# Attention scored over pairs of heads, 64 queries of each per tile, in a fused attention and two-MoE kernel

## The chip, the cores and the metric

The kernel runs on one core of a Trainium2 chip. The metric is device time in microseconds: 1187.81 us is the median of three runs of the kernel before (1185.43 to 1188.58). Engines are called as the profile calls them: PE is the matrix engine, PEld its weight loads, DVE the vector engine, ACT the scalar engine, POOL the third elementwise engine, and SP the engine that issues all DMAs here. Each engine works through its own list of instructions in order, so an instruction that waits holds up everything behind it on that engine.

## The reference, cut to what matters

Causal attention in blocks of 64 positions over 4 batches of 8 heads, 576 positions and head size 64, then two gated layers (512 to 1536 to 512) over all 2304 tokens.

```python
scores = (1/sqrt(64)) * q @ k.T                     # per head, 576 x 576
mask = (pos[:, None] // 64) >= (pos[None, :] // 64) # whole 64-blocks
attn = softmax(where(mask, scores, -1e9))           # row maximum taken off first
x = attn @ v                                        # -> (2304, 512)
x = (x @ w_a) * (x @ w_b) @ w_out                   # layer 1
xn = x / rms(x) * rms_g                             # layer 2
out = silu(xn @ w_gate) * (xn @ w_val) @ w_out2
```

## The kernel before

**Numbers in two halves.** float32 matmuls are made of matmuls in the type F32R. A float32 operand is split in a high part (a copy in F32R) and a low part (the operand less the copy). The two layers (`moe`, L444 to L446 and L471 to L473) use three products per tile. Products of two plain F32 operands also occur: for the eight heads of batch 0 ("plain" heads) the values are not split and L375 works on F32.

**Attention, head by head.** `score(m, i)` takes 128 queries (64 in the last of five tiles) against all keys up to the last that any of them may see: 128, 256, 384, 512 and 576 keys (576 in two halves of 288). Queries (`qh`, `ql`) and keys (`kk`) are split by `make_qk` (L252 to L258); since the head size is 64, `kk` holds the high part of the keys in one half of its 128 rows and the low part in the other. Each score tile is two matmuls (L289 with `qh`, L290 with `ql`) into a PSUM tile `s` (or `mm`). DVE writes the masked value over the 64 by 64 corner that the earlier 64 queries may not see (L293) and reduces the row maximum (L295; L298 and L299 for halves). ACT takes the exponential and its row sum (L301). L311 and L312 make reciprocals of the sums, and POOL scales the probabilities `p` (L315). `p_transposes` turns them in 128 by 128 pieces (L336, with `ident` or `swap`), and the result leaves PSUM as a high part `ph` (ACT, L353) and a low part `pl` (DVE, L354); for plain heads as one copy. `values` multiplies with the values `vv` (L375) and adds up the two halves into `xf` (L386, L387).

**Weights.** They arrive as 64-bit words in 72 pieces of 512 KB. `prepare()` takes a piece: a load into a staging tile `st` (three buffers, `stage_loads`, L154), `decode` on ACT, DVE and POOL (L131 to L135), a split (L97, L107) and a write of the result to DRAM, from where later blocks fetch it (L188, L192). The pieces of layer 1 are all decoded before or during the first token block, those of layer 2 in the background of blocks 1 to 4.

**Order.** First attention of batch 0 runs alone, with nine weight pieces between its steps. Then five token blocks of layer 1 follow (512, then four times 448 tokens; 432 matmuls each), then the five of layer 2. Attention of batches 1 to 3 is mixed into blocks 0 to 2: after each step of `moe` the attention stream is stepped while its accounted cost is below a share (`PACE`) of that of the block, with a higher priority (`AHEAD`). Attention that the next block needs and that isn't issued by the last part of a block is issued there in one go (`before_last`). A scheduler then orders each engine's list by priority and by when it takes operands to be ready, so the lists differ from the order of the code.

Of the kernel before, what the change touches and what calls it, by code (L numbers as in the profile page):

```python
# [17 lines left out]
MASKED = -1000000000.0  # L18
# [5 lines left out]
Q_HI = "aad"  # L24
# [22 lines left out]
def tile_attention_moe_moe(  # L47
# [40 lines left out]
    swap = const.tile([P, P], F32, name="swap")  # L88
# [60 lines left out]
    def stage_loads(n):  # L149
        while len(staged) + prepared[0] < min(n, len(w_pieces)):  # L150
            i = len(staged) + prepared[0]
            layer, kind, f, y = w_pieces[i]
            st = stage.tile([P, 4 * P], I64, tag="st", name="st", bufs=3)
            sp.dma_start(out=st, in_=(w_ab if kind == "ab" else w_o)[layer][f, y])  # L154
            staged[i] = st

    def prepare():
# [4 lines left out]
        stage_loads(i + 3)  # L162
# [27 lines left out]
    def fetch_o(layer, i):  # L190
# [13 lines left out]
    ]  # L204
    PLACE, PART = {}, [0, 0]
    for part, pieces in GROUPS:
        for j, i in pieces:
            PLACE.setdefault(j, (part, PART[part]))
            PART[part] += tw(i)

    def attention(pools, x_of, done):

        ap, ap2, ps_s, ps_t = pools
        NH = B * H
        n_copy = [0]
        q_raw, k_raw, v_raw, qk, vv, pp, st, pt = {}, {}, {}, {}, {}, {}, {}, {}

        def rows(m):
            hh = m % 2
            return slice(hh * D, hh * D + D), slice(D - hh * D, P - hh * D)  # L220

        def plain(m):

            return m < H

        def load(m):
            if m >= NH:
                return
            b, h = divmod(m, H)
            if h % 2 == 0:  # L230
                t = ap2.tile([P, S], F32, tag="kr", name="kr", bufs=1)
                sp.dma_start(out=t, in_=k[b, h // 2])
                k_raw[m] = k_raw[m + 1] = t
            t = ap2.tile([P, S], F32, tag="qr", name="qr")
            sp.dma_start(out=t[0:D, :], in_=q[b, h])
            sp.dma_start(out=t[D:P, :], in_=q[b, h])
            q_raw[m] = t
            t = ap2.tile([P, NTILE, D], F32, tag="vr", name="vr")
            sp.dma_start(out=t[:, 0:LAST_TILE, :], in_=v[b, h][:, 0:LAST_TILE, :])

            sp.dma_start(out=t[P - R:P, LAST_TILE, :], in_=v[b, h][0:R, LAST_TILE, :])
            sp.dma_start(out=t[0:P - R, LAST_TILE, :], in_=v[b, h][R:P, LAST_TILE, :])
            v_raw[m] = t

        def make_qk(m):
            if m >= NH:
                return
            r, z = rows(m)
            qr, kr = q_raw.pop(m), k_raw.pop(m)
            qh = ap2.tile([P, S], F32R, tag="qh", name="qh")  # L250
            kk = ap2.tile([P, S], F32R, tag="kk", name="kk")
            act.activation(kk[r, :], kr[r, :], AF.Copy, scale=SCALE)  # L252
            copy(eng[Q_HI[min(m // H, len(Q_HI) - 1)]], qh, qr)
# [5 lines left out]
            qk[m] = (qh, ql, kk)  # L259

        def make_vv(m):
            if m >= NH:
                return
            t = v_raw.pop(m)
            if plain(m):
                vv[m] = t
                return
            o = ap2.tile([P, NTILE, P], F32R, tag="vv", name="vv")
            hi, lo = o[:, :, 0:D], o[:, :, D:P]
            copy(pool, hi, t)  # L270
            pool.tensor_tensor(lo, t, hi.bitcast(F32), ALU.subtract)
            vv[m] = o

        def score(m, i):

            qh, ql, kk = qk[m]
            w = tw(i)
            nk = i * P + w
            o = nk - P
            if m not in st:  # L280
                st[m] = ap2.tile([P, 16], F32, tag="st", name="st")
            s = st[m]
            pi = ap2.tile([P, nk], F32, tag=f"p{i}", name=f"p{i}")
            pp[m, i] = pi
# [7 lines left out]
            if w == P:  # L292
                dve.memset(pss[-1][0:64, nk - 64 - halves[-1][0]:nk - halves[-1][0]], MASKED)  # L293
            if len(halves) == 1:
                dve.tensor_reduce(s[:, i:i + 1], pss[0][:, 0:nk], axis=AX.X, op=ALU.max, negate=True)  # L295
            else:
                for x, (a, z) in enumerate(halves):
                    dve.tensor_reduce(s[:, 14 + x:15 + x], pss[x][:, 0:z - a], axis=AX.X, op=ALU.max)  # L298
                dve.tensor_reduce(s[:, i:i + 1], s[:, 14:16], axis=AX.X, op=ALU.max, negate=True)  # L299
            for x, (a, z) in enumerate(halves):  # L300
                act.activation(  # L301
                    pi[:, a:z], pss[x][:, 0:z - a], AF.Exp, bias=s[:, i:i + 1], scale=1.0,
                    accum_out=s[:, 5 + i + x:6 + i + x],
                )
# [11 lines left out]
            return sum(2 * max(107.0, (z - a) / 2.4) for a, z in halves)

        def p_transposes(m):
            pt[m] = []
            at = [0, 0]  # L320
            for part, pieces in GROUPS:
                ps = ps_t()
                n, cost = 0, 0.0
                first, rest = [], []
                for j, i in pieces:

                    if tw(i) == P:
                        rest.append((n, j, i, ident))
                    elif n >= P - R:
                        first.append((n - (P - R), j, i, ident))  # L330
                    else:
                        first.append((n, j, i, swap))
                    n += tw(i)
                for o, j, i, perm in first + rest:
                    a = min(j * P, S - P)
                    pe.transpose(ps[:, o:o + P], pp[m, i][:, a:a + P], perm)  # L336
                    cost += P / 1.2
                if at[part] == 0:
                    kinds = ["hl"[m % 2]] if plain(m) else "hl"
                    dt = F32 if plain(m) else F32R  # L340
                    pt[m].append(
                        [ap.tile([P, PART[part]], dt, tag=f"p{x}{part}", name=f"p{x}{part}") for x in kinds]
                    )
                both = [t[:, at[part]:at[part] + n] for t in pt[m][part]]
                at[part] += n
                if plain(m):
                    n_copy[0] += 1
                    if n_copy[0] % 2 == 0:
                        dve.tensor_copy(both[0], ps[:, 0:n])
                    else:  # L350
                        gate["act"] = act.activation(both[0], ps[:, 0:n], AF.Copy)
                else:
                    gate["act"] = act.activation(both[0], ps[:, 0:n], AF.Copy)  # L353
                    dve.tensor_tensor(both[1], ps[:, 0:n], both[0].bitcast(F32), ALU.subtract)  # L354
                yield cost
            for i in tiles:
                del pp[m, i]

        def values(m):
            b, h = divmod(m, H)  # L360
            p = h // 2
            x = x_of(b)
            r, z = rows(m)
            cost = 0.0
            for a, e in ((0, R), (R, S)):
                ps = ps_t()
                seq = []
                for j in tiles:
                    q0 = max(a, j * P)
                    if q0 < e:  # L370
                        part, n = PLACE[j]
# [348 lines left out]
```

## Time and profile before

| | |
|---|---|
| median of 3 runs | 1187.81 us |
| the profiled execution | 1193.02 us, of which the span is 1191.2 us |
| PE busy | 1132.8 us, 95% of the span |
| DVE, ACT, POOL busy | 710.1, 529.5 and 489.1 us (60, 44 and 41%) |
| mean granted clock of PE | 0.97 of full |

The span is best read by position in the PE list. Counting the matmuls of the layers (L444 to L446, L471 to L473), the 48th starts at 111.62 us, the 432nd is done at 270.77 (end of token block 0), the 864th at 395.80 (block 1), the 912th at 429.65, the 1344th at 563.75 and the 1440th at 589.55. The last attention matmul lies ahead of the 1344th. From 589.55 to the end there is no attention.

### The profile page before, as it was taken

Reading aid. Unit: us, or ns where it says so; the run is one execution under the profiler, and the core shown is the slowest. Engines: PE = TensorE matmul, PEld = TensorE weight load, DVE = VectorE, ACT = ScalarE, POOL = GpSimd, SP = SyncE. Lnnn points to the kernel's source line nnn. Section 1 sums busy time; section 2 is a strip of 40 time slices with the busy share of each in tenths; the row PEclk is TensorE's granted clock in tenths of the full one; section 3 lists DMA queues with packets and bytes.
Section 4 is the critical chain, followed back from the end, with each engine's and each line's share of the span. In section 5 each row is a group of like instructions: output and inputs, shape, how many; then the busy total and the mean of one; then the engine's idle time right before and its main releaser. Section 6 shows DMA issues by size and latency. Waiting matters only on the chain.

```text
span 1191.2 us, 16081 instructions
## 1 busy us (share of the span) xinstructions
PE 1132.8 (95%) x5578; PEld 992.0 (83%) x5578; DVE 710.1 (60%) x1411; ACT 529.5 (44%) x1174; POOL 489.1 (41%) x474
## 2 busy tenths in 40 slices
PE   7888888989999889998999999999999999999998
PEld 5566667769989779898899998888999999999997
DVE  7869799997777787778945523323624534433222
ACT  7758776765655666556533312312312312211211
POOL 6748767776636565546535202112012112112110
PEclk9898988999999889999899999999999999999999
DMA  5436575879777667658898956655765765765760
GB/s 177 147 113 217 192 260 173 311 251 335 261 239 240 229 234 234 230 203 309 310 412 323 341 198 246 224 195 191 279 228 198 280 221 204 256 214 209 255 227 35
DMA packets 65905, 279.98 MB, mean 235 GB/s; under 512 B 12064, under 2 KB 22304, under 8 KB 45344
## 3 DMA queue, kind: packets, MB, share of 16 engines
q1 hardware_dynamic: 65824, 278.95, 66.3%
q8 instruction: 44, 0.72, 0.2%
q14 instruction: 37, 0.30, 0.1%
HBM read 231.74 MB, written 47.19 MB: 234 GB/s over the span
## 4 chain that ended last, share of the span: by engine, by line
PE 67%; DVE 9%; ACT 4%; DMA 3%; POOL 2%; issue 2%; DVEq 0%; POOLq 0%; ACTq 0%
PE mm L445 14%; PE mm L446 14%; PE mm L444 14%; PE mm L471 7%; PE mm L472 7%; PE mm L473 7%; PE t L336 2%; PE t L375 2%; POOL x L135 1%; DVE kk L254 1%; DVE x L133 1%; PE s L289 1%; DVE st L134 1%; PE s L290 1%; DVE pl L354 1%
## 5 line engine op out<-in xcount | busy, mean ns | idle before, releaser
L444 PE MATMUL mm<-xh,ab 128*128 128x448 f32 (+1 forms) x960 | 360.2, 377 | 6.1 <-DVE xf L387 2.1
L446 PE MATMUL mm<-xh,ab 128*128 128x448 f32 (+1 forms) x960 | 358.7, 374 | 0.3 <-POOL ab L107 0.2
L445 PE MATMUL mm<-xl,ab 128*128 128x448 f32 (+1 forms) x960 | 358.3, 373 | 0.0
L107 POOL TENSOR_TENSOR hl<-g,hh 128x448 fp32r<-128x448 f32 (+1 forms) x80 | 99.4, 1243 | 425.1 <-ACT hh L97 424.5
L444 PEld LDWEIGHTS mm<-xh,ab 128*128 128x128 f32 x960 | 181.5, 189 | 26.3 <-ACT ab L97 2.9
L446 PEld LDWEIGHTS mm<-xh,ab 128*128 128x128 f32 x960 | 181.6, 189 | 19.9 <-POOL ab L107 0.4
L445 PEld LDWEIGHTS mm<-xl,ab 128*128 128x128 f32 x960 | 181.9, 190 | 18.3
L471 PE MATMUL mm<-hh,o 128*128 128x448 f32 (+1 forms) x480 | 182.3, 381 | 5.0 <-ACT hh L97 3.5
L472 PE MATMUL mm<-hh,o 128*128 128x448 f32 (+1 forms) x480 | 179.4, 374 | 0.0
L473 PE MATMUL mm<-hl,o 128*128 128x448 f32 (+1 forms) x480 | 169.1, 374 | 0.9 <-POOL hl L107 0.9
L97 ACT ACTIVATE hh<-g 128x448 fp32r<-128x448 f32 (+1 forms) x120 | 70.5, 588 | 204.2 <-DVE g L456 203.7
L315 POOL TENSOR_SCALAR p<-p,st 128x128 f32<-128x128 f32 (+4 forms) x160 | 106.5, 677 | 106.4 <-DVE st L312 63.9
L456 DVE SCALAR_TENSOR_TENSOR g<-mm,asb 128x448 f32<-128x448 f32 (+1 forms) x120 | 76.1, 635 | 117.5 <-PE mm L446 116.6
L135 POOL TENSOR_TENSOR x<-x,st 128x512 uint32<-128x512 uint32 x72 | 104.9, 1461 | 70.3 <-DVE st L134 27.1
L453 DVE SCALAR_TENSOR_TENSOR asb<-mm,asb 128x448 f32<-128x448 f32 (+1 forms) x60 | 38.2, 636 | 144.7 <-ACT asb L452 144.7
L301 ACT ACTIVATE p<-s,st 128x128 f32<-128x128 f32 (+2 forms) x171 | 88.5, 520 | 69.3 <-DVE st L295 40.7
L481 DVE SCALAR_TENSOR_TENSOR acc<-mm,acc 128x448 f32<-128x448 f32 (+1 forms) x120 | 69.9, 627 | 70.6 <-PE mm L473 70.5
L471 PEld LDWEIGHTS mm<-hh,o 128*128 128x128 f32 x480 | 90.9, 190 | 18.2 <-ACT hh L97 5.3
L473 PEld LDWEIGHTS mm<-hl,o 128*128 128x128 f32 x480 | 90.3, 189 | 11.7 <-POOL hl L107 1.7
L452 ACT ACTIVATE asb<-mm 128x448 f32<-128x448 f32 (+1 forms) x60 | 33.4, 556 | 148.1 <-PE mm L446 148.1
L472 PEld LDWEIGHTS mm<-hh,o 128*128 128x128 f32 x480 | 91.3, 190 | 9.1
L336 PE MATMUL t<-ident,p 128*128 128x128 f32 x416 | 73.2, 295 | 3.1 <-POOL p L315 2.9
(99 smaller groups left out, 1645.2 us busy)
## 6 DMA issues: line engine op xcount, KB each, us to landing
ab<-wab SPq DMA_DIRECT2D x108, 1024.0 KB, 6.0
o<-wo SPq DMA_DIRECT2D x36, 1536.0 KB, 6.9
st<-in_w_ab_dram SPq DMA_DIRECT2D x48, 512.0 KB, 4.5
wab<-ab SPq DMA_DIRECT2D x12, 1024.0 KB, 4.5
st<-in_w_o_dram SPq DMA_DIRECT2D x24, 512.0 KB, 4.9
wab<-bg SPq DMA_DIRECT2D x24, 512.0 KB, 7.0
qr<-in_q_dram SPq DMA_DIRECT2D x64, 144.0 KB, 3.8
wo<-o SPq DMA_DIRECT2D x4, 1536.0 KB, 6.2
```

Of the source, the lines that this page charges most:

```text
L107: eng_lo.tensor_tensor(lo, src, hi.bitcast(F32), ALU.subtract)
L135: pool.tensor_tensor(x, x, lo, ALU.add)
L301: act.activation(pi[:, a:z], pss[x][:, 0:z - a], AF.Exp, bias=s[:, i:i + 1], scale=1.0, accum_out=s[:, 5 + i + x:6 + i + x],)
L315: pool.tensor_scalar(pi, pi, s[:, 5 + y:6 + y], 1.0, ALU.mult, ALU.mult)
L336: pe.transpose(ps[:, o:o + P], pp[m, i][:, a:a + P], perm)
L444: pe.matmul(ps[:, 0:n], wh[:, a:z], xh[:, c, 0:n], start=(c == 0), stop=False)
L445: pe.matmul(ps[:, 0:n], wh[:, a:z], xl[:, c, 0:n], start=False, stop=False)
L446: pe.matmul(ps[:, 0:n], wl[:, a:z], xh[:, c, 0:n], start=False, stop=(c == KC - 1))
L456: dve.scalar_tensor_tensor(g, ps[:, 0:n], UNSCALE, asb, ALU.mult, ALU.mult)
L471: pe.matmul(ps[:, 0:n], wh, hh, start=(y == 0), stop=False)
L472: pe.matmul(ps[:, 0:n], wl, hh, start=False, stop=False)
L473: pe.matmul(ps[:, 0:n], wh, hl, start=False, stop=(y == TF - 1))
```

## The change

Two neighbouring heads are scored together. A tile now holds 64 queries of one head and the same 64 queries of the other, in `qz`: rows 0 to 63 hold the first head's queries with zeros in the second head's columns, and rows 64 to 127 the reverse, so that one matmul against the keys of both heads (128 rows) scores both. Nine tiles per pair (64 to 576 keys) take the place of ten; all 128 rows of a tile see the same keys, so there is no mask. Scores are single F32 matmuls: queries and keys are not split. Queries arrive in runs of 64 numbers. The probability tiles `pp` are allocated once. A pair is worked in two parts (query blocks 0 to 5, and 6 to 8), the values of all batches are split, and 25 pieces per pair are transposed, where it was 30. The staging tile `st` has two buffers, and in the first stage a weight piece is prepared at every 9th step.

```diff
-            st = stage.tile([P, 4 * P], I64, tag="st", name="st", bufs=3)
+            st = stage.tile([P, 4 * P], I64, tag="st", name="st", bufs=2)
...
-        stage_loads(i + 3)
+        stage_loads(i + 2)
...
+    Q = P // 2
+    NQ = S // Q
+    PARTS = (range(0, 6), range(6, NQ))
+    SCORED = (tuple(PARTS[0]), (NQ - 1, *range(6, NQ - 1)))
+    NORM = ({3: (0, 4), 5: (4, 6)}, {NQ - 1: (NQ - 1, NQ), NQ - 2: (6, NQ - 1)})
...
+        PLACE.append([(j, b) for j in range(NTILE) for b in blocks_of(part, j)])
...
+        qz = [ap.tile([P, NQ, 2, Q], F32, name=f"qz{x}") for x in range(2)]
...
+        pp = [ap.tile([P, P * (b // 2 + 1)], F32, name=f"pp{b}") for b in range(NQ)]
...
-            sp.dma_start(out=t[0:D, :], in_=q[b, h])
-            sp.dma_start(out=t[D:P, :], in_=q[b, h])
+            for hh in range(2):
+                sp.dma_start(
+                    out=qz[m % 2][hh * D:hh * D + D, :, hh, :],
+                    in_=q[b, 2 * h + hh].rearrange("d (n q) -> d n q", q=Q),
+                )
...
-            dve.scalar_tensor_tensor(
-                kk[z, :], kr[r, :], SCALE, kk[r, :].bitcast(F32), ALU.mult, ALU.subtract
-            )
-            ql = ap2.tile([P, S], F32R, tag="ql", name="ql")
-            pool.tensor_tensor(ql, qr, qh.bitcast(F32), ALU.subtract)
+            t = ks[m] = ap2.tile([P, S], F32, tag="ks", name="ks")
+            act.activation(t, k_raw.pop(m), AF.Copy, scale=SCALE)
...
-                pe.matmul(ps[:, 0:z - a], qh[:, o:nk], kk[:, a:z], start=True, stop=False)
-                pe.matmul(ps[:, 0:z - a], ql[:, o:nk], kk[:, a:z], start=False, stop=True)
+                pe.matmul(ps[:, 0:z - a], qz[m % 2][:, b], ks[m][:, a:z], start=True, stop=True)
...
-                dve.memset(pss[-1][0:64, nk - 64 - halves[-1][0]:nk - halves[-1][0]], MASKED)
...
+                for x, (j, b) in enumerate(group):
+                    pe.transpose(ps[:, x * P:(x + 1) * P], pp[b][:, j * P:(j + 1) * P], ident)
+                n = len(group) * P
+                hi, lo = [t[:, at * P:at * P + n] for t in pt[u]]
+                gate["act"] = act.activation(hi, ps[:, 0:n], AF.Copy)
+                dve.tensor_tensor(lo, ps[:, 0:n], hi.bitcast(F32), ALU.subtract)
...
+                        for t in pt[u]:
+                            t = t.rearrange("p (n h q) -> p n h q", h=2, q=Q)
+                            seq.append((t[:, at:at + len(bs), hh, :], j, (bs[0] - b0) * Q))
...
+                    pe.matmul(
+                        ps[:, o:n], vv[m][:, hh, j, :], src, start=(y == 0), stop=(y == len(seq) - 1)
+                    )
...
-        if n % 16 == 15 and prepared[0] < 2 * TF + TF:
+        if n % 9 == 8 and prepared[0] < 2 * TF + TF:
```

In the changed kernel the score matmul is L263, the transpose L298, the values matmul L324, the layer matmuls L390 to L392 and L417 to L419, and the load of `st` L151.

The first place is the PE list early in token block 2 (after the 888th matmul of the layers). In the kernel before, nine rows there are the end of a product of the layer, transposes and the scores of the next head, each tile twice:

```order
L446 MATMUL mm<-xh,ab 128x448
L336 MATMUL t<-ident,p_4365 128x128
L336 MATMUL t<-ident,p_4395 128x128
L289 MATMUL s<-kk,qh 128x128
L290 MATMUL s<-kk,ql 128x128
L289 MATMUL s<-kk,qh 128x256
L290 MATMUL s<-kk,ql 128x256
L289 MATMUL s<-kk,qh 128x384
L290 MATMUL s<-kk,ql 128x384
```

In the changed kernel, at the same place in block 2 (after the 881st):

```order
L298 MATMUL t<-ident,pp_138 128x128
L298 MATMUL t<-ident,pp_139 128x128
L298 MATMUL t<-ident,pp_140 128x128
L298 MATMUL t<-ident,pp_141 128x128
L263 MATMUL s<-ks,qz_133 128x448
L263 MATMUL s<-ks,qz_133 128x512
L392 MATMUL mm<-xh,ab 128x448
L390 MATMUL mm<-xh,ab 128x448
L391 MATMUL mm<-xl,ab 128x448
```

A score tile is one row where it was two, and two tiles stand between transposes and products of the layer. Between the 864th and the 912th matmul of the layers the PE list held 26 score matmuls, 30 transposes and 13 value matmuls; now it holds 4, 12 and 20.

The second place is the SP list in token block 0, where weights are loaded and decoded. Before, around the fourth write of a decoded weight (`wab_3`):

```order
L154 DMA st<-in_w_ab_dram 128x512
L232 DMA kr<-in_k_dram 128x576
L154 DMA st<-in_w_o_dram 128x512
L235 DMA qr<-in_q_dram 64x576
L236 DMA qr<-in_q_dram 64x576
L180 DMA wab_3_73<-ab 128x2048
L154 DMA st<-in_w_ab_dram 128x512 x2
```

Now, around the same write:

```order
L235 DMA kr<-in_k_dram 128x576
L238 DMA vr<-in_v_dram 128x320 x2
L151 DMA st<-in_w_o_dram 128x512
L151 DMA st<-in_w_ab_dram 128x512
L177 DMA wab_3_73<-ab 128x2048
L151 DMA st<-in_w_ab_dram 128x512
L151 DMA st<-in_w_o_dram 128x512
```

The loads of weights stand closer together, and a load of `st` now waits for the tile two loads earlier to be decoded, where it waited for the tile three loads earlier. Over the whole program the lists have 985 rows on DVE (1286 before), 834 on ACT (888), 343 on POOL (399) and 343 on SP (460).

## Rows read from the trace of the kernel before

**Rows 1.** Windows, whole core by stage: busy us (count) of PE PEld DVE ACT POOL, PEclk, DMA, GB/s

```profile
0.00:111.62 111.62, 91.30 (x412) 64.00 (x412) 88.88 (x247) 81.61 (x207) 75.15 (x85) 0.89 0.50 160
111.62:270.77 159.15, 141.42 (x661) 111.95 (x660) 144.33 (x281) 110.13 (x250) 119.88 (x108) 0.94 0.68 238
270.77:395.80 125.03, 124.17 (x699) 114.74 (x698) 93.41 (x228) 73.54 (x186) 72.69 (x81) 1.00 0.75 261
395.80:429.65 33.85, 26.14 (x118) 21.97 (x117) 23.28 (x61) 20.64 (x52) 19.69 (x24) 0.80 0.62 213
429.65:563.75 134.10, 129.27 (x710) 116.95 (x709) 104.19 (x232) 79.32 (x195) 74.91 (x81) 0.99 0.72 249
563.75:589.55 25.80, 23.24 (x99) 20.25 (x97) 23.95 (x24) 13.83 (x25) 13.32 (x10) 0.87 0.82 300
589.55:1191.20 601.65, 597.23 (x2889) 542.12 (x2887) 232.02 (x343) 150.38 (x264) 113.42 (x89) 1.00 0.66 238
```
**Rows 2.** Timeline of PE in block 1: start us, us, engine, line, operation, count

```profile
280.12 0.37 PE L444 MATMUL mm<-xh,ab 128*128 128x448 f32 x1
...
282.76 0.37 PE L445 MATMUL mm<-xl,ab 128*128 128x448 f32 x1
...
284.00 0.39 PE L375 MATMUL t<-ph,vv 128*128 128x512 f32 x1
...
284.66 0.30 PE L289 MATMUL s<-kk,qh 128*128 128x288 f32 x1
...
284.93 0.37 PE L375 MATMUL t<-pl,vv 128*128 128x448 f32 x1
...
285.79 0.44 PE L336 MATMUL t<-ident,p 128*128 128x128 f32 x2
...
296.29 1.14 PE L336 MATMUL t<-ident,p 128*128 128x128 f32 x9
...
297.27 0.27 PE L336 MATMUL t<-swap,p 128*128 128x128 f32 x1
...
298.14 0.39 PE L289 MATMUL s<-kk,qh 128*128 128x512 f32 x1
...
298.60 0.36 PE L473 MATMUL mm<-hl,o 128*128 128x448 f32 x1
```
**Rows 3.** Timeline of PE, values of a plain head of batch 0

```profile
77.59 2.80 PE L375 MATMUL t<-ph,vr 128*64 128x512 f32 x10
80.32 0.44 PE L336 MATMUL t<-ident,p 128*128 128x128 f32 x2
```
**Rows 4.** Timeline of PE at the start of block 2, the wait ahead in brackets

```profile
405.18 0.33 PE L289 MATMUL s<-kk,qh 128*128 128x128 f32 x1 [2.65 <-ACT p L301]
...
418.58 1.07 PE L444 MATMUL mm<-xh,ab 128*128 128x448 f32 x3 [1.98 <-DVE xh L99]
```
**Rows 5.** Groups by line and shape: busy us, mean ns, idle before and its releasers

```profile
L135 POOL TENSOR_TENSOR x<-x,st 128x512 uint32<-128x512 uint32 x72 | 104.9, 1461 | 70.3 <-DVE st L134 27.1 <-DVE x L133 22.2 <-issue 6.1
...
L134 DVE SCALAR_TENSOR_TENSOR st<-st 128x512 uint32<-128x512 uint32 x72 | 67.8, 952 | 5.0 <-ACT st L131 5.0
...
L254 DVE SCALAR_TENSOR_TENSOR kk<-kr,kk 64x576 fp32r<-64x576 f32 x32 | 43.1, 1347 | 10.2 <-ACT kk L252 9.3
...
L295 DVE TENSOR_REDUCE st<-s 128x1 f32<-128x512 f32 x32 | 21.8, 682 | 0.4
...
L293 DVE MEMSET s<- 64x64 f32 x114 | 12.4, 112 | 13.7 <-PE s L290 12.8
...
L295 DVE TENSOR_REDUCE st<-s 128x1 f32<-128x128 f32 x25 | 7.2, 288 | 0.7
```
**Rows 6.** Waits of SP's queue: line, releaser, us in total, times, longest us

```profile
SPq L154 <- POOL x L135: 149.4, 60, 6.6
```
**Rows 7.** Page, part 6: DMA issues, count, KB each, median us to landing

```profile
st<-in_w_ab_dram SPq DMA_DIRECT2D x48, 512.0 KB, 4.5
...
qr<-in_q_dram SPq DMA_DIRECT2D x64, 144.0 KB, 3.8
```

More of the change, by code (lines that the diff above doesn't have):

```diff
@@ L211, in attention, with blocks_of @@
+    def blocks_of(part, j):
+        return [b for b in PARTS[part] if b >= 2 * j]
+    PLACE = []
+    for part in range(2):
+        PLACE.append([(j, b) for j in range(NTILE) for b in blocks_of(part, j)])
     def attention(pools, x_of, done):
         ap, ap2, ps_s, ps_t = pools
[L214 to L220, printed above, removed]
@@ L226, in load @@
         def load(m):
-            if m >= NH:
+            if m >= NP:
                 return
[L229 to L234, printed above, removed]
-            sp.dma_start(out=t[0:D, :], in_=q[b, h])
-            sp.dma_start(out=t[D:P, :], in_=q[b, h])
-            q_raw[m] = t
@@ L238, in load @@
[L238 to L246, printed above, removed]
-                return
[L248 to L253, printed above, removed]
-            dve.scalar_tensor_tensor(
-                kk[z, :], kr[r, :], SCALE, kk[r, :].bitcast(F32), ALU.mult, ALU.subtract
-            )
-            ql = ap2.tile([P, S], F32R, tag="ql", name="ql")
-            pool.tensor_tensor(ql, qr, qh.bitcast(F32), ALU.subtract)
-            qk[m] = (qh, ql, kk)
+            b, h = divmod(m, H // 2)
@@ new lines, in load @@
+            for hh in range(2):
[3 more added lines that the diff above has]
+                )
+            t = k_raw[m] = ap2.tile([P, S], F32, tag="kr", name="kr", bufs=1)
+            sp.dma_start(out=t, in_=k[b, h])
+            t = v_raw[m] = ap2.tile([P, 2, NTILE, D], F32, tag="vr", name="vr")
+            for hh in range(2):
+                sp.dma_start(out=t[:, hh], in_=v[b, 2 * h + hh])
@@ L316, in score @@
[L316 to L321, printed above, removed]
-                ps = ps_t()
[L323 to L365, printed above, removed]
+                t = s[:, 10 + b:11 + b]
+                dve.tensor_tensor(t, t, s[:, 11 + b:12 + b], ALU.add)
+            for norm in NORM:
+                if b in norm:
+                    b0, b1 = norm[b]
+                    t = s[:, 10 + b0:10 + b1]
+                    dve.tensor_scalar(t, t, 1e-9, None, ALU.add)
+                    dve.reciprocal(t, t)
+                    for y in range(b0, b1):
+                        t = pp[y][:, 0:Q * (y + 1)]
+                        pool.tensor_scalar(t, t, s[:, 10 + y:11 + y], 1.0, ALU.mult, ALU.mult)
@@ new lines, in score, with p_transposes @@
+            return sum(max(107.0, (z - a) / 0.6) for a, z in halves)
+        def p_transposes(u):
+            m, part = divmod(u, 2)
+            places = PLACE[part]
+            pt[u] = [ap.tile([P, len(places) * P], F32R, tag=f"p{x}{part}", name=f"p{x}{part}") for x in "hl"]
+            for at in range(0, len(places), 4):
+                ps = ps_t()
+                group = places[at:at + 4]
+                for x, (j, b) in enumerate(group):
[4 more added lines that the diff above has]
+                dve.tensor_tensor(lo, ps[:, 0:n], hi.bitcast(F32), ALU.subtract)
+                yield n / 1.2
@@ L366, in values @@
+        def values(u):
+            m, part = divmod(u, 2)
+            batch, h = divmod(m, H // 2)
+            x = x_of(batch)
+            b0 = PARTS[part][0]
+            n = len(PARTS[part]) * Q
+            for hh in range(2):
+                r, z = slice(hh * D, hh * D + D), slice(D - hh * D, P - hh * D)
                 ps = ps_t()
                 seq = []
[L368 to L371, printed above, removed]
-                        n += q0 - j * P
-                        seq += [(src[:, n:n + e - q0], j, q0) for src in pt[m][part]]
@@ L392, in attention @@
+            del pt[u]
+            if part == 1:
+                del vv[m]
+                done[batch] = done.get(batch, 0) + 2
         load(0)
         yield 0.0
-        make_qk(0)
+        make_k(0)
         load(1)
         yield 0.0
-        for m in range(NH + 2):
-            if m >= 2:
-                yield values(m - 2)
-            sc = list(tiles) if m < NH else []
-            ct = p_transposes(m - 1) if 1 <= m <= NH else iter(())
+        for u in range(2 * NP + 2):
+            m, part = divmod(u, 2)
+            if u >= 2:
+                yield from values(u - 2)
+            sc = list(SCORED[part]) if m < NP else []
+            ct = p_transposes(u - 1) if 1 <= u <= 2 * NP else iter(())
```

109 lines of the change are left out of this document (38 added, 71 removed), and 4 rows, old and new, of the table GROUPS.

## The prediction

> **What bounds the kernel now.** I read the stages first, cut at positions of the PE list [rows 1]. From 589.55 us on PE is busy for 597 of 602 us at full clock and holds no attention, so half of the span is out of the change's reach. Ahead of it lie six stretches: A (attention of batch 0, to 111.62 us), B (token block 0, 159.15 us), C (block 1, 125.03), L (the 48 layer matmuls that open block 2, 33.85), D (up to the 1344th, 134.10) and E (to the 1440th, 25.80). A busy PE is pipelined work, so next I took from PE's timeline what an instruction costs when PE isn't kept waiting, from start to start, at the full clock. Thirteen layer matmuls on 448 columns run from 280.12 to 282.76: 0.203 us each (0.222 for 512 columns, by 1/2.4 ns per further column). Nine transposes take 0.98: 0.109 each. A score tile in two halves of operand takes 0.27 for 288 columns and 0.46 for 512; for 384, 256 and 128 I read 0.35, 0.235 and 0.22, the last from the floor that the transposes show, 0.109 per instruction. That is 1.80 us per head in twelve matmuls. The values of a head with split operands take 1.79 less the score pair within, 1.52, plus two short ones of 0.11: 1.74 in twelve [rows 2]. Ten F32 records of a plain head, 1536 columns, take 2.73, so F32 costs 1.78 ns a column, four times the 0.45 of an F32R product; with its two short ones a plain head's values take 3.0 us in six matmuls [rows 3].
>
> With the counts of the order before (score, transpose, value and layer matmuls) the PE work and the rest, which is waiting or lower clock, are: A 118, 137, 60, 48: 69.0 of 111.6; B 86, 105, 84, 384: 121.7 of 159.2; C 80, 103, 83, 432: 122.9 of 125.0; L 26, 30, 13, 48: 18.8 of 33.9; D 74, 105, 96, 432: 124.1 of 134.1; E 96 layer matmuls: 19.5 of 25.8. So 476 us of work stand in 589.6, and 113.5 are lost: 42.6, 37.4, 2.1, 15.1, 10.0, 6.3. Only C is bound by PE. In B DVE is busy for 144 of 159 us, the fullest engine [rows 1]. In L PE waits 2.65 us for an exponential and 1.98 for the operands of block 2, which need the last heads of batch 2; the granted clock of L is 0.80, so part of it ran at 1.2 GHz after such waits, where C, without them, had 1.00 [rows 1, 4].
>
> **The change part by part.**
>
> *Scores.* A pair of heads took 24 matmuls, 3.6 us. Now it takes ten F32 matmuls on 64 to 576 columns, 2880 in all: at 1.78 ns 5.13 us [rows 3], plus 0.1 because the 64-column one has two weight loads at the floor of 0.109 [rows 2]. 5.2 us, +1.6. That weight loads of 128 F32 columns hide behind F32 products isn't shown (the plain heads load 64). From both sides: all hidden 5.1, or all twenty bare at 0.109 7.3; I take 5.2, the nearer row.
>
> *Transposes.* 25 for 30 per pair: -0.55.
>
> *Values.* Batches 1 to 3: 32 matmuls per pair, two heads with 384, 256 and 128 columns and four times 192, and 64, each twice: 2 x (0.35 + 0.235 + 0.22 + 0.80 + 0.22) is 3.6 us, where two heads took 3.5: +0.1. Batch 0: 3.6 for 6.0, -2.4. Moving operands now come in runs of 64 numbers with gaps of 64; no row shows such a read. Between nothing and twice the time (+3.6 us per pair) I take nothing.
>
> So a pair costs PE +1.15 us in batches 1 to 3 and -1.35 in batch 0: 12 x 1.15 - 4 x 1.35, +8 us in all. Alone, this makes the kernel slower.
>
> *DVE.* Per pair the low half of the keys goes (two of 1.347 us), eight masks of 0.112, and reductions of 3712 columns become 2880: between 0.288 us at 128 and 0.682 at 512 I interpolate 5.7 us before and 4.5 now [rows 5]. That is 4.8 us less per pair, some 75 over 16 pairs, and small operations on row sums besides. POOL loses the low part of the queries, ACT their high part and some exponentials. Batch 0 gains the low parts of its probabilities, which it didn't make; its sum on DVE still falls.
>
> *What PE waits for.* With the new order the counts are: A 56, 116, 140, 48; B 34, 96, 117, 384; C 48, 113, 139, 432; L 4, 12, 20, 48; D 18, 63, 96, 432; E 96. At 0.52 per score, 0.109 and 0.112 the work is 68, 126, 141, 15, 115 and 19.5, 484 in all. Attention is brought forward: batch 2 is done at the 768th layer matmul, before block 2 starts at the 865th, where it was still open, and no attention is left after the 1152nd. Term by term:
> - A: scores of 11.2 heads lie in it where there were 9.8, on about the same work. Its loss is a chain through all engines; I take 34 for 42.6: 102 us. Ends 92 and 120.
> - B: 3.4 pairs at 4.8 us take some 16 us from DVE's 144: 128, beside 126 on PE. At DVE's share of 0.907 that would be 140. Two engines are now equally full, and `st` has a buffer less, so I take 148. Ends 132 and 175.
> - C: PE-bound, 141 and 3 lost: 144. It is the stage that gets slower, by 19, since it now does more of the attention.
> - L: 15 and 2 lost: 17. The heads that it waited for are done. Ends 15 and 26.
> - D: 115 and 3: 118. The 10 lost lay at the same kind of place, the entry to block 3. Ends 115 and 127.
> - E: 19.5 and 1.5: 21. Ends 19.5 and 26.
>
> Sum 550 for 589.6: -39.5. The profiled execution took 1193.02, with the span at 1191.2; it would come to 1153.5. It lies 5.2 over the median of the runs shown, so the forecast is 1187.8 less 39.5: 1148 us.
>
> *Loads.* The queries come once, in runs of 256 bytes, where they came twice in rows of 2304; a load of 144 KB took 3.8 us [rows 7], and a pair lasts over 15 us in every stage, so there is cover for one of twice or thrice that. The Trainium skill (DMA: Bandwidth & Descriptors, Specifications) speaks against the new form: it gives 512 bytes as the least transfer for the full rate, with a read-modify-write below. By that rule the halved bytes cost as much as before and the sum keeps its value; by bytes alone DMA would be a little freer in B and D; no row here times runs of 256 bytes, and neither moves a term, since the queries are a small part of the traffic.
>
> **The rivals.**
>
> *The staging buffers decide B (slower).* SP already waits 149.4 us in 60 loads for POOL's L135 to free an `st` tile [rows 6]. With two, a load starts only when the tile two before is decoded. A cycle is 4.5 us of landing [rows 7] and the decoding, at least 1.46 + 0.95 for its two last steps [rows 5] and about 5 with ACT and queueing; two tiles share it: 4.8 us per piece, 27 pieces in B, 128 us, just hidden. It decides above 148/27 = 5.5 us per piece, a decoding of 6.5. Ahead of a late piece ACT's list stands still, and the exponentials behind it. At 9.5 us of decoding B takes 189, and with its waits passed to C the kernel is at 1192. For it: DVE's L134 has a mean of 0.95 us in a full stage. Against it: those engines carry less. 6%.
>
> *The waits don't shrink.* If they are latencies of the chains and not load, 113.5 stay on 484 of work: +8, 1196 us. For it: A's chains are as long as before. Against it: L's loss has a named cause that the order takes away. 4%.
>
> *PE becomes the bound in A and B too.* Losses of 25 and 10 in place of 34 and 22: 1127 us. For it: C's 2.1 lost in 125. Against it: A has no layer work to fill gaps. 20%.
>
> *Half the gain.* A and B stay at 112 and 159, only L, D and E gain: 1169. 17%.
>
> **How the numbers follow.** The forecast has 50%, with 1136 to 1160 as its own range; the rivals have 20, 17, 6 and 4; 3% stay for gapped operands or bare weight loads, which could take the whole gain. The range of 8 in 10 reaches from the fast rival to half the gain with some room: 1120 to 1178. 0.3% of the median (3.6 us) is about what can be told from no change: faster 0.87, same 0.03, slower 0.10.
>
> **What would show it.** Right: score records in twos per tile that start 0.46 us apart at 512 columns, PE at over 98% of C, no attention wait of over 2 us at the start of block 2, and the 1440th layer matmul near 550 us. Wrong: the first steps of decode on ACT waiting for `st` loads in B for 20 us or more; C over 150 us, which would mean that F32 products cost over 1.78 ns a column; value matmuls on 384 columns starting over 0.2 us apart, which would be the gapped reads; A over 112.

## The result and the profile after

The changed kernel takes 1149.49 us, the median of four runs (1148.49 to 1150.71), where the kernel before took 1187.03 on the same occasions: a ratio of 0.968 (95% interval 0.967 to 0.970). The forecast was 1148.

The windows of the changed kernel's profiled execution, cut at the same layer matmuls (48th, 432nd, 864th, 912th, 1344th, 1440th), answer to [rows 1]; columns are the busy time (and count) of PE, PEld, DVE, ACT and POOL, the granted clock, the DMA share and GB/s:

```profile
0.00:103.39 103.39, 82.26 (x417) 61.11 (x417) 83.41 (x195) 78.69 (x208) 66.90 (x90) 0.97 0.57 180
103.39:252.98 149.59, 138.57 (x679) 111.13 (x678) 120.94 (x216) 101.60 (x226) 96.35 (x89) 0.97 0.71 245
252.98:393.90 140.92, 139.56 (x773) 123.82 (x773) 87.36 (x199) 84.56 (x213) 69.26 (x83) 1.00 0.77 256
393.90:408.96 15.06, 15.06 (x87) 13.42 (x86) 8.89 (x21) 9.46 (x24) 9.08 (x9) 1.00 0.79 259
408.96:526.33 117.37, 116.07 (x628) 104.54 (x627) 67.67 (x135) 65.60 (x145) 58.52 (x59) 1.00 0.79 284
526.33:546.25 19.92, 19.92 (x100) 18.41 (x98) 14.47 (x17) 11.23 (x20) 5.86 (x6) 1.00 1.01 422
546.25:1148.10 601.85, 596.30 (x2889) 542.08 (x2887) 228.08 (x340) 143.82 (x252) 104.71 (x83) 1.00 0.64 230
```

A is 8.2 us shorter, B 9.6, L 18.8, D 16.7 and E 5.9; C is 15.9 longer; from the 1440th matmul on nothing changed (601.85 and 601.65). The reader should compare DVE in B, 120.9 of 149.6 us where it was 144.3 of 159.2, and the clock: 0.80 in L before, 1.00 now. C is the price: PE has more columns to do there and next to nothing to wait for (busy for 139.6 of 140.9 us).

The profiled execution of the kernel before took 1193.0 us, 6 more than its median of 1187.0; that of the changed kernel took 1149.9, 0.4 more. So the stretches are 43 us shorter in all, the medians 37.5, and it isn't known in which stretch the 6 us lie.

What a score costs now stands in PE's timeline in block 1 (start, us, line, operation, count; two records per F32 matmul), to be set beside the pairs L289 and L290 of [rows 2]:

```profile
306.29 0.37 PE L390 MATMUL mm<-xh,ab 128*128 128x448 f32 x1
306.49 0.91 PE L263 MATMUL s<-ks,qz 128*128 128x448 f32 x2
306.90 0.72 PE L391 MATMUL mm<-xl,ab 128*128 128x448 f32 x1
307.45 1.02 PE L263 MATMUL s<-ks,qz 128*128 128x512 f32 x2
...
308.52 0.37 PE L390 MATMUL mm<-xh,ab 128*128 128x448 f32 x1
```

From one L390 to the next lie three layer matmuls (0.61 us) and two score tiles on 960 columns: 2.23 - 0.61 = 1.62, or 1.69 ns a column. Each starts right behind the matmul ahead of it, so the weight loads of 128 columns are hidden: that of the first tile begins at 306.29, 0.20 us ahead of its matmul. What PE and ACT still waited for in B (waits: total, times, longest):

```profile
PE s L263 <- ACT pp L272: 9.6, 7, 2.6
...
ACT st L128 <- DMA st<-in_w_ab_dram: 7.9, 10, 1.6
...
ACT st L128 <- DMA st<-in_w_o_dram: 4.2, 4, 1.4
```

### The profile page after: what moved, and what is told of

The parts are those of the page before. It is cut to its first block, busy times and chain, and to the rows that moved or that the text cites. A ratio compares the mean times of both kernels' runs of the same rounds, so it can differ in the third digit from the quotient of the medians.

```text
span 1148.1 us, 15321 instructions
## 1 busy us (share of the span) xinstructions
PE 1107.7 (96%) x5562; PEld 974.5 (85%) x5562; DVE 610.8 (53%) x1118; ACT 495.0 (43%) x1086; POOL 410.7 (36%) x414
## 4 chain that ended last, share of the span: by engine, by line
PE 51%; DVE 0%; ACT 0%; DVEq 0%; issue 0%
PE mm L390 11%; PE mm L391 11%; PE mm L392 11%; PE mm L417 6%; PE mm L418 6%; PE mm L419 6%; DVE acc L427 0%; PE r L522 0%; PE r L521 0%; ACT hh L94 0%; DVE g L402 0%; DVEq L660 0%
## 5 line engine op out<-in xcount | busy, mean ns | idle before, releaser
L391 PE MATMUL mm<-xl,ab 128*128 128x448 f32 (+1 forms) x960 | 362.1, 377 | 1.0 <-POOL xl L104 1.0
L390 PE MATMUL mm<-xh,ab 128*128 128x448 f32 (+1 forms) x960 | 360.2, 377 | 1.4 <-DVE xh L96 1.1
L392 PE MATMUL mm<-xh,ab 128*128 128x448 f32 (+1 forms) x960 | 360.7, 376 | 0.0
L390 PEld LDWEIGHTS mm<-xh,ab 128*128 128x128 f32 x960 | 181.2, 189 | 22.5 <-DVE xh L96 1.5
L392 PEld LDWEIGHTS mm<-xh,ab 128*128 128x128 f32 x960 | 180.9, 188 | 20.6 <-issue 1.1
L417 PE MATMUL mm<-hh,o 128*128 128x448 f32 (+1 forms) x480 | 181.1, 379 | 1.8 <-ACT hh L94 1.4
L419 PE MATMUL mm<-hl,o 128*128 128x448 f32 (+1 forms) x480 | 170.3, 375 | 0.0
L132 POOL TENSOR_TENSOR x<-x,st 128x512 uint32<-128x512 uint32 x72 | 97.8, 1358 | 130.1 <-DVE x L130 57.2
L263 PE MATMUL s<-ks,qz 128*128 128x384 f32 (+4 forms) x284 | 98.2, 438 | 17.1 <-ACT pp L272 17.0
L287 POOL TENSOR_SCALAR pp<-pp,st 128x64 f32<-128x64 f32 (+3 forms) x144 | 86.7, 617 | 56.3 <-DVE st L284 32.8
L417 PEld LDWEIGHTS mm<-hh,o 128*128 128x128 f32 x480 | 90.6, 189 | 14.1 <-ACT hh L94 2.1
L419 PEld LDWEIGHTS mm<-hl,o 128*128 128x128 f32 x480 | 90.3, 188 | 10.3 <-issue 0.2
L272 ACT ACTIVATE pp<-s,st 128x288 f32<-128x288 f32 (+8 forms) x142 | 71.3, 505 | 39.2 <-DVE st L266 26.3
```

Source lines behind the costliest of these rows:

```text
L132: pool.tensor_tensor(x, x, lo, ALU.add)
L263: pe.matmul(ps[:, 0:z - a], qz[m % 2][:, b], ks[m][:, a:z], start=True, stop=True)
L272: act.activation(pi[:, a:z], pss[x][:, 0:z - a], AF.Exp, bias=s[:, b:b + 1], scale=1.0, accum_out=s[:, 10 + b + x:11 + b + x],)
L287: pool.tensor_scalar(t, t, s[:, 10 + y:11 + y], 1.0, ALU.mult, ALU.mult)
L390: pe.matmul(ps[:, 0:n], wh[:, a:z], xh[:, c, 0:n], start=(c == 0), stop=False)
L391: pe.matmul(ps[:, 0:n], wh[:, a:z], xl[:, c, 0:n], start=False, stop=False)
```

## The experiments

Times of the stretches in us from the profiled execution of each kernel, all cut at the same layer matmuls (to within four of them, up to 1.2 us), then the median and the ratio to the kernel before on the same chip.

| | A | B | C | L | D | E | median us | ratio to before |
|---|---|---|---|---|---|---|---|---|
| before | 111.6 | 159.2 | 125.0 | 33.9 | 134.1 | 25.8 | 1187.0 | |
| changed | 103.4 | 149.6 | 140.9 | 15.1 | 117.4 | 19.9 | 1149.5 | 0.968 |
| e1 third staging buffer | 99.8 | 150.3 | 135.0 | 12.4 | 132.6 | 20.3 | 1155.2 | 0.973 (0.969 to 0.976) |
| e2 before, two buffers | 103.0 | 159.2 | 127.4 | 28.7 | 136.0 | 25.6 | 1181.0 | 0.994 (0.992 to 0.997) |
| e3 DVE work put back | 108.6 | 154.5 | 136.0 | 12.4 | 126.3 | 20.3 | 1161.0 | 0.977 (0.974 to 0.981) |
| e4 one-pass scores | 102.8 | 135.8 | 123.9 | 14.0 | 111.9 | 19.9 | 1110.6 | 0.937 (0.933 to 0.941) |
| e5 before, F32, 64 rows | 111.4 | 153.9 | 153.1 | 24.6 | 149.9 | 20.2 | 1218.3 | 1.026 (1.023 to 1.028) |
| e6 before, paced ahead | 109.5 | 169.7 | 123.4 | 21.4 | 134.2 | 25.1 | 1186.2 | 1.000 (0.998 to 1.001) |
| e7 every 16th step | 96.1 | 145.9 | 139.3 | 15.1 | 119.1 | 19.9 | 1138.2 | 0.959 (0.956 to 0.962) |
| e8 three score banks | 115.7 | 147.8 | 127.7 | 14.1 | 140.4 | 20.1 | 1168.7 | 0.984 (0.981 to 0.988) |
| e9 before, F32, 128 rows | 106.6 | 151.2 | 135.9 | 21.6 | 137.3 | 21.2 | 1176.9 | 0.991 (0.989 to 0.993) |
| e10 every 24th step | 94.9 | 148.4 | 144.1 | 15.1 | 118.2 | 19.9 | 1142.0 | 0.961 (0.958 to 0.963) |
| e11 e7 and third buffer | 100.9 | 153.7 | 134.4 | 12.4 | 133.5 | 20.3 | 1161.0 | 0.978 (0.975 to 0.981) |
| e12 e7 and e4 | 103.3 | 160.0 | 116.9 | 11.6 | 115.9 | 20.1 | 1133.1 | 0.954 (0.952 to 0.956) |

**e1, staging buffers in the changed kernel.**

```diff
-            st = stage.tile([P, 4 * P], I64, tag="st", name="st", bufs=2)
+            st = stage.tile([P, 4 * P], I64, tag="st", name="st", bufs=3)
-        stage_loads(i + 2)
+        stage_loads(i + 3)
```

> The changed kernel with a third staging buffer for weights again (and the lookahead of three that goes with it). Theory (part of what is still lost in token block 0 is ACT's list standing at loads of st that start too late; it waits 13.8 us for them there, where it was 4.6 before): block 0 falls from 149.6 us to some 142 to 146, the rest keeps its time, 1143 to 1147 us against 1149.5. Rival (the loads are hidden, since DVE and PE are full anyway): block 0 within 1.5 us of 149.6, 1148 to 1151.

B and D of this run:

```profile
99.77:250.06 150.29, 142.18 (x690) 113.36 (x688) 125.05 (x223) 103.32 (x232) 99.95 (x94) 0.97 0.71 243
...
397.44:530.04 132.60, 126.42 (x676) 112.47 (x675) 86.01 (x161) 74.44 (x171) 69.08 (x71) 0.99 0.77 274
```

My theory fell and the rival held for B: ACT's waits for `st` there went from 13.8 to 8.7 us and block 0 kept its 150 us, so those waits were not what ended last. The whole got slower all the same: the new order leaves more attention to block 2 (130 of 160 score tiles were done at the 864th layer matmul, where it had been 138), and D pays 15.2 us, more than A, C and L save.

**e2, the same in the kernel before.**

```diff
-            st = stage.tile([P, 4 * P], I64, tag="st", name="st", bufs=3)
+            st = stage.tile([P, 4 * P], I64, tag="st", name="st", bufs=2)
-        stage_loads(i + 3)
+        stage_loads(i + 2)
```

> The kernel before with two staging buffers for weights, the one part of the change that takes something away. Theory (nearly hidden behind the decode work on DVE, 5.5 us per piece): block 0 grows by 2 to 6 us, 1189 to 1193 us against 1187. Rival (the loads decide block 0): it grows by 12 us or more, to 1199 or above.

Neither: block 0 stayed at 159.2 to the tenth, and the kernel became 6 us faster, by A (at a granted clock of 0.95, where it had 0.89) and L. So the staging buffers don't bound block 0 in either kernel, and the lost buffer was no cost of the change.

**e3, the load on DVE.** Added behind the scaling of the keys, into a tile that nothing reads:

```diff
+            for hh in range(2):
+                r = slice(hh * D, hh * D + D)
+                dve.scalar_tensor_tensor(
+                    junk[r, :], kr[r, :], SCALE, t[r, :], ALU.mult, ALU.subtract
+                )
```

> The changed kernel with the DVE work of the key split put back: two operations on 64 x 576 per pair, written to a tile that nothing reads, so no chain gets longer, 16 x 2.7 = 43 us of DVE in all. Theory (the stages of attention of batch 0 and of token block 0 gained because DVE's load fell): these two grow by 5 to 9 us each, blocks 1 and 2 keep their time, 1159 to 1167 us in all. Rival (their loss is latency of the chains, not load): under 3 us in all, 1149 to 1152.

A and B of the run, and the group of the added operations (busy us, mean ns, idle before and its releaser):

```profile
0.00:108.58 108.58, 83.81 (x401) 62.66 (x401) 87.93 (x200) 73.96 (x197) 65.35 (x82) 0.92 0.53 163
108.58:263.06 154.48, 142.15 (x697) 113.86 (x695) 127.31 (x233) 105.01 (x237) 103.01 (x96) 0.97 0.70 243
```

```profile
L249 DVE SCALAR_TENSOR_TENSOR junk<-kr,ks 64x576 f32<-64x576 f32 x32 | 30.6, 958 | 8.7 <-ACT ks L246 8.3
```

11.5 us over the changed kernel, within the theory's range, and A and B grew as it said, by 5.2 and 4.9. Blocks 1 and 2 didn't keep their times: C fell by 4.9 and L by 2.7, D grew by 8.9, because eight more score tiles were left for block 2, as in e1; together these make 1.3. The amount is not load alone: the operations took 0.96 us each, 30.6 in all (43 had been expected), DVE also stood 8.3 us waiting for ACT's keys, as the split had made it do, and the granted clock of A fell from 0.97 to 0.92.

**e4, the price of F32 on PE.** The low parts of queries and keys are left out; the queries are copied once per pair:

```diff
+        qr = ap.tile([P, NQ, 2, Q], F32R, name="qr")
...
-            t = ks[m] = ap2.tile([P, S], F32, tag="ks", name="ks")
+            t = ks[m] = ap2.tile([P, S], F32R, tag="ks", name="ks")
...
+                copy(pool, qr, qz[m % 2])
...
-                pe.matmul(ps[:, 0:z - a], qz[m % 2][:, b], ks[m][:, a:z], start=True, stop=True)
+                pe.matmul(ps[:, 0:z - a], qr[:, b], ks[m][:, a:z], start=True, stop=True)
```

> The changed kernel with scores as one product in F32R (queries copied once per pair by POOL, 1152 columns; the low parts of queries and keys are left out, so scores are rounded): ten matmuls per pair at 0.109 to 0.23 us, 1.7 us in place of 5.2. Theory (blocks 1 and 2 are bound by PE, and scores cost 1.78 ns a column there): these fall by 7 pairs x 3.5 = 25 us; batch 0 alone and block 0 give back 10 to 18 more; 1106 to 1117 us. Rival (the attention chain or ACT bounds blocks 1 and 2 already): they fall by less than 10 us, and the whole stays above 1130.

```profile
0.00:102.77 102.77, 78.55 (x361) 64.54 (x362) 81.22 (x195) 77.41 (x208) 74.63 (x96) 0.83 0.62 182
102.77:238.57 135.80, 125.63 (x651) 102.36 (x650) 118.09 (x218) 102.26 (x234) 102.06 (x93) 1.00 0.76 263
238.57:362.42 123.85, 122.28 (x714) 113.30 (x713) 85.52 (x192) 81.19 (x205) 74.18 (x86) 1.00 0.85 294
```

As the theory had it. C, L and D fall by 23.6 us (25 expected), so there PE's columns are time one for one. B falls by 13.8, about what 3.8 pairs at 3.5 us save: it is bound by PE as well now. A falls by 0.6 although some 20 us of PE work left it; its clock went to 0.83. That doesn't show a chain through the other engines as the bound of A: in these ten microseconds, nearly all at the lower level, PE itself was busy for 9.57, DVE and ACT for little over half:

```profile
50.00:60.00 10.00, 9.57 (x37) 8.49 (x38) 5.46 (x15) 5.63 (x18) 7.51 (x7) 0.53 0.52 190
```

A mean of 0.83 between the levels of 1.2 and 2.4 GHz is some 35 us of A at 1.2 GHz (the changed kernel's 0.97 is some 6), so part of what the lighter scores freed was paid back there. What A would take at the full clock isn't known.

**e5 and e9, no split but still head by head.** e5 uses the head's 64 rows; e9 puts zeros in the other 64 rows of the queries, which it so loads once and not twice, and keeps both heads' keys:

```diff
-                pe.matmul(ps[:, 0:z - a], qh[:, o:nk], kk[:, a:z], start=True, stop=False)
-                pe.matmul(ps[:, 0:z - a], ql[:, o:nk], kk[:, a:z], start=False, stop=True)
+                pe.matmul(ps[:, 0:z - a], qh[:, o:nk], kk[:, a:z], start=True, stop=True)
...
+            qk[m] = (qr[r, :], None, kk[r, :])      # e5
+            qk[m] = (qr, None, kk)                  # e9
```

> The kernel before, head by head with masks and 128 queries per tile, but with scores as one F32 matmul per tile on the 64 rows of the head (no split of queries and keys): 1856 columns per head at 1.78 ns, 3.3 us for 1.8, and 1.35 us of DVE and 1.5 of POOL less per head. Theory (PE's price eats what DVE gives back; only two heads in one matmul, which halves the F32 columns, makes it pay): batch 0 alone and block 0 gain 5 to 15 us together, blocks 1 and 2 lose 13 heads x 1.5 = 20 less what block 2's start gains, 1183 to 1197 us. Rival (dropping the split's work is the gain, pairs or not): 1170 or less.

> The run without a split, head by head, again, but with zeros in the other 64 rows of the queries and the keys of both heads beside them, so that every score matmul has 128 rows and the columns stay the same. There a tile of 512 columns took 1.15 us and one of 288 took 0.76, a quarter of a microsecond over 1.78 ns a column. Theory (a matmul on 64 rows among those on 128 doesn't hide its two weight loads): tiles fall to 0.91 and 0.51, block 1 from 153 to about 141 us, the whole to 1185 to 1198. Rival (the extra belongs to F32 tiles of a single head or to where they stand): block 1 stays over 149 and the whole over 1210.

A tile of 288 columns in e5, among layer matmuls, and the same in e9; then the loads of their weights (PEld), two of e5 and one of e9:

```profile
307.46 0.36 PE L437 MATMUL mm<-xl,ab 128*128 128x448 f32 x1
307.75 0.75 PE L282 MATMUL s<-kk,qr 64*128 64x288 f32 x2
308.43 0.47 PE L438 MATMUL mm<-xh,ab 128*128 128x448 f32 x1
308.74 0.36 PE L436 MATMUL mm<-xh,ab 128*128 128x448 f32 x1
```

```profile
296.25 0.37 PE L438 MATMUL mm<-xl,ab 128*128 128x448 f32 x1
296.45 0.65 PE L283 MATMUL s<-kk,qr 128*128 128x288 f32 x2
296.72 0.58 PE L439 MATMUL mm<-xh,ab 128*128 128x448 f32 x1
297.14 0.36 PE L437 MATMUL mm<-xh,ab 128*128 128x448 f32 x1
```

```profile
307.75 0.29 PEld L282 LDWEIGHTS s<-kk,qr 64*128 64x128 f32 x2 [0.31 <-issue]
308.43 0.19 PEld L438 LDWEIGHTS mm<-xh,ab 128*128 128x128 f32 x1 [0.39 <-issue]
...
296.25 0.39 PEld L283 LDWEIGHTS s<-kk,qr 128*128 128x128 f32 x2
```

From L437 to the second next layer matmul in e5 are 1.28 us, less two of them (0.203 each) 0.87 for the tile. In e9 from L438 to the second next are 0.89, less two of them 0.48. The columns are the same; 0.39 us belong to the 64 rows. In e9 the weight load begins 0.20 us ahead of its matmul; in e5 it begins only with its matmul, and so does the load for the 128-row matmul behind the tile. (The 0.76 and 1.15 us in the text of e9 were taken to the next layer matmul and miss this second part.) It is a price per run of such tiles and not per tile: two tiles in a row, of 128 and 256 columns, took 1.04 us in e5 (from 332.83) and 0.65 in e9 (from 340.06), again 0.39 apart. The score tiles of e5 stand in 142 such runs, which makes 55 us. 79 of these are in C, L and D, 31 us, and these stretches are 33 us longer than in e9; in A and B, which have 63, only 8 us of some 25 show. That is why e5 came out 21 us above its theory's range. (The text of e5 is wrong in one point: pairs don't halve the F32 columns. They go from 3712 to 2880 per pair.) B and C of e9:

```profile
106.61:257.77 151.16, 139.90 (x654) 108.69 (x653) 131.32 (x270) 106.58 (x245) 110.15 (x105) 0.99 0.71 252
257.77:393.68 135.91, 135.91 (x720) 119.99 (x718) 89.30 (x231) 80.55 (x201) 73.53 (x90) 1.00 0.70 241
```

The theory of e9 held on the tiles, and the whole came out 8 us below its range: dropping the split alone is worth 10 us, since A, B, L and E gain 30 us from lighter engines and C and D pay 14. From there to the change's 1149.5 lie 27 us. The pairs bring 22% fewer F32 columns, no masks and fewer reductions; but the split values of batch 0, the cadence and the order differ as well, and no run parts these.

**e6, order alone.**

```diff
-PACE, AHEAD = (0.47, 0.53, 0.53), (50, 200, 200)
+PACE, AHEAD = (0.60, 0.60, 0.60), (50, 200, 200)
```

> The kernel before with attention paced ahead of the layers (share 0.60 in each block, where it was 0.47 and 0.53), the order part by itself without any lighter load. Theory (attention was late at the start of block 2 because its engines were loaded, not because of the pace): that stretch keeps over 8 of its 15 us of loss, 1180 to 1191 us. Rival (the new order is the gain): it goes to under 20 us and the whole to 1175 or less.

```profile
109.46:279.16 169.70, 146.91 (x699) 118.81 (x698) 149.77 (x307) 117.92 (x271) 125.71 (x115) 0.93 0.66 231
...
402.51:423.90 21.39, 18.45 (x88) 16.47 (x87) 19.74 (x40) 12.53 (x30) 13.35 (x15) 0.84 0.87 303
```

The whole stayed (theory), but not in the way that it said: L fell from 33.9 to 21.4, and B, into which the attention was pulled, grew by 10.5, with DVE at 149.8 us. So the wait at block 2 reads as a debt of loaded engines: paid earlier it cost the same.

**e7 and e10, the cadence of weight pieces.**

```diff
-        if n % 9 == 8 and prepared[0] < 2 * TF + TF:
+        if n % 16 == 15 and prepared[0] < 2 * TF + TF:      # e7; e10: n % 24 == 23
```

> The changed kernel with weight pieces at every 16th step of batch 0, as before the change. Theory (the pieces are the same nine, only placed later): within 4 us, 1146 to 1154; what batch 0 gains comes back ahead of block 0. Rival (the closer cadence is what made batch 0 shorter): 1156 or more.

> The changed kernel with weight pieces at every 24th step of batch 0 (four of the nine in it, five behind it). Theory (pieces among the attention of batch 0 slow its chain more than they would cost behind it, where DVE and ACT would otherwise wait for PE): batch 0 a further 0 to 4 us shorter than with every 16th, and block 0 the same or up to 4 longer, 1134 to 1143 us. Rival (there is a best cadence near 16, since the last pieces then hold up the first layer matmuls): 1144 or more.

A, B and C of e7:

```profile
0.00:96.09 96.09, 77.09 (x405) 56.75 (x405) 73.59 (x179) 70.13 (x189) 57.29 (x80) 1.00 0.51 156
96.09:242.00 145.91, 138.34 (x695) 110.73 (x693) 123.99 (x228) 107.31 (x244) 102.52 (x97) 1.00 0.78 270
242.00:381.26 139.26, 139.26 (x772) 123.80 (x771) 88.16 (x203) 85.07 (x216) 71.78 (x85) 1.00 0.79 265
```

For e7 theory and rival were both off. Every 16th step is 11 us faster than the change as it was made, and the fastest kernel here that keeps the arithmetic: A runs 7.3 us shorter at a full clock, and B, which has the later pieces to do, doesn't pay but gains 3.7, at a full clock too (0.97 in the change). Every 24th held its theory (A 1.2 us shorter still, B 2.5 longer); it came out 4 us slower than every 16th, but the intervals overlap.

**e8, banks.**

```diff
-    pss = attn.enter_context(tc.tile_pool(name="pss", bufs=2, space=PSUM, side="right"))
-    pst = attn.enter_context(tc.tile_pool(name="pst", bufs=3, space=PSUM, side="right"))
+    pss = attn.enter_context(tc.tile_pool(name="pss", bufs=3, space=PSUM, side="right"))
+    pst = attn.enter_context(tc.tile_pool(name="pst", bufs=2, space=PSUM, side="right"))
```

> The changed kernel with three PSUM banks for scores and two for transposes and values (it has two and three). PE waits 9.6 us in block 0 and 7 in batch 0 for an exponential that frees a bank of scores. Theory (those waits are what is left of PE's loss): these two stretches fall by 3 to 7 us each, 1137 to 1145 us. Rival (the wait moves to transposes and values, which now have two banks): no gain or a loss, 1149 or more.

```profile
0.00:115.68 115.68, 88.89 (x407) 67.09 (x407) 80.20 (x196) 78.09 (x208) 66.31 (x89) 0.88 0.51 160
...
405.31:545.71 140.40, 133.42 (x715) 119.56 (x714) 77.36 (x163) 74.12 (x176) 59.86 (x66) 0.96 0.67 232
```

The rival: 19 us slower. A grew by 12.3 us at a clock of 0.88, and D by 23, with attention left over for it (129 score tiles done at the 864th). In A PE's waits for tiles of transposes and values went from 5.6 to 10.3 us, and those for a bank of scores didn't shrink (6.9 and 8.0): transposes and values need the third bank more than scores do.

**e11 and e12, do gains add up?** e11 joins the edits of e1 and e7, e12 those of e4 and e7.

> Every 16th step and three staging buffers together. Theory (the third buffer saves nothing in block 0 and its order leaves more attention to block 2, as with every 9th step, where it cost 4 to 6 us): 1140 to 1148 us. Rival (with the pieces later the loads of st are late, so the buffer is worth something): below 1135.

> Every 16th step and scores as one product in F32R (without the low parts of queries and keys, so rounded). Theory (the two gains lie in different stretches, batch 0 and the PE-bound blocks, and add up): 1110.5 less 8 to 13, 1097 to 1103 us. Rival (with PE lighter, batch 0 is bound by the chain and its clock falls whatever the cadence): 1107 or more.

Neither adds up. e11 lost all that the cadence had gained, and 12 us beside, beyond its theory; as in e1, 130 score tiles were done at the 864th layer matmul, and D is as long as there. e12 is 23 us slower than e4 alone, as its rival's number had it. The clock of A did fall, to 0.80 where e7 had 1.00, but against e4 the loss lies in B. Its A and B, and two of PE's waits in B:

```profile
0.00:103.33 103.33, 77.19 (x358) 62.05 (x358) 75.44 (x182) 71.38 (x194) 67.37 (x87) 0.80 0.53 153
103.33:263.36 160.03, 139.27 (x683) 112.08 (x682) 135.06 (x254) 115.38 (x268) 118.21 (x111) 0.96 0.72 245
```

```profile
PE mm L392 <- ACT ab L94: 4.9, 4, 1.8
...
PE mm L394 <- POOL ab L104: 2.4, 2, 1.6
```

PE now waits in B for decoded weights, which it did hardly at all in e4, and DVE is at 135.1 us there (118.1 in e4). Of the 24 us that B grew, PE's idle time makes 10.6. The other 13.6 are busy time, with 32 more matmuls and a clock of 0.96 where e4 had 1.00. Pieces moved into a block with less PE work may cost time that F32 scores (e7) cover; that is argued from these rows and not tried by itself.

## Why the prediction was right

Term by term, forecast and measured: A 102 and 103.4, B 148 and 149.6, C 144 and 140.9, L 17 and 15.1, D 118 and 117.4, E 21 and 19.9; sum 550 and 546.3. The closeness of the whole, 1148 and 1149.5, is in part luck: the stretches fell by 43.3 us where 39.6 had been forecast, and the median by 37.5, because the profile of the kernel before lay so far above its median.

- *PE work by counts.* Right. C, D and E have next to nothing but work in them, and e4 shows that a score column there is time. The size of the F32 column was 1.69 ns, not 1.78, which makes 1.2 us in C (4.8 pairs of 2880 columns). A layer matmul on 512 columns was put at 0.222 us and takes 0.227, which makes 2 us in A and B. Weight loads on 128 rows hide, as I had chosen; e5 shows that the doubt was in place, since those on 64 rows next to 128 don't. The gapped reads of the values cost nothing that could be seen: matmuls on 384 columns start 0.17 to 0.18 us apart, at the price that the sum had taken from reads without gaps.

```profile
311.16 0.33 PE L324 MATMUL t<-ph,vv 128*128 128x384 f32 x1
311.33 0.34 PE L324 MATMUL t<-pl,vv 128*128 128x384 f32 x1
311.51 0.29 PE L324 MATMUL t<-ph,vv 128*128 128x256 f32 x1
```

- *Where the gain comes from.* Right in the main: e3 puts 10 of the 18 us that A and B had gained back into them by DVE, and e6 shows that attention had earlier without a lighter load gains nothing. L and D gained most, and as named, with no wait of PE over 1.0 us left at the entry to blocks 2 and 3.
- *Waiting or lower clock.* The sum keeps the two in one loss. Layer matmuls on 512 columns start 0.43 us apart at the lower level (the first two rows, where the granted clock is 0.50) and 0.23 at the higher (the last two, at 1.00), both in block 0 of the changed kernel:

```profile
200.06 0.63 PE L392 MATMUL mm<-xh,ab 128*128 128x512 f32 x1
200.49 0.63 PE L390 MATMUL mm<-xh,ab 128*128 128x512 f32 x1
...
204.04 0.39 PE L418 MATMUL mm<-hh,o 128*128 128x512 f32 x1
204.26 0.40 PE L419 MATMUL mm<-hl,o 128*128 128x512 f32 x1
```

  By the mean clocks of the windows, PE stood at 1.2 GHz for some 67 us up to the 1440th layer matmul before (25 in A, 19 in B, 14 in L) and for some 15 now (6 in A, 9 in B). Each of these microseconds holds back at most 0.47 us of work, so up to 24 of the 43 us may have come by way of the clock. No run parts it from the waits.
- *B's 22 lost.* Right in size, wrong in one reason. Part of it I gave to the buffer that `st` lost. e1 gives it back and B stays; e2 takes it away and B stays. PE is busy there for 138.6 of 149.6 us, DVE for 120.9, less than the 128 that I had.
- *A's 34 lost.* Right in size by cancellation, which is luck. The sum has no term for the cadence of nine steps; by e7 it costs 7.3 us in A and 11 in all. Without it the change would have been at 1138.
- *Loads of queries.* A load took 4.2 us for 3.8 [rows 7]:

```profile
qz<-in_q_dram SPq DMA_DIRECT2D x32, 144.0 KB, 4.2
```

  Hidden, as said, whether the runs of 256 bytes are slow or not.

Of the rivals, the staging buffers deciding B, and waits that don't shrink, are refuted by e1 and by the windows; so is half the gain, since A and B did get shorter. PE as the bound was half true of B (e4: B followed PE); of A, where its forecast was 10 us too short, e4 leaves it open because the clock fell.

## What to carry to other kernels

Count instructions by stretch in the new order, price them from start to start in a stretch where the engine waits for nothing, and keep work and loss apart: work could be summed here to about two per cent (C, L, D and E), and only the losses needed judgement. Where PE waits for loaded engines, giving PE more columns to take work off the others pays until PE is full; past that each column is time. Small edits (a buffer, a bank, a cadence) change the scheduler's order, moved the time by 5 to 20 us here and didn't add up, so each needs its own run in the kernel in which it is to stand. Read the granted clock of a stretch before the length of a stretch is put down to an engine.

## What was not expected of the hardware

- F32 score tiles on 64 rows among matmuls with 128 cost 0.39 us more, once per run of such tiles, than the same columns on 128 rows, half of which are zeros (0.87 and 0.48 us for 288 columns). Padding with zeros was faster by 41 us in the whole (e5 and e9; e9 also has one load of queries less per head and a fill with zeros more).
- A stretch whose work on PE was cut got no shorter, at a lower granted clock: A in e4 took 102.8 us at 0.83 where it had taken 103.4 at 0.97; a part of it ran at 1.2 GHz.
